# A decode kernel with two passes over a KV cache: the per-row layer chain as column products, cut into one-engine steps between K and V chunks

## The chip, the cores and the metric

One core of a Trainium2 chip runs the whole program. The metric is device time of one execution in microseconds (us), the median of several runs. A profile is one execution; its span is about 2 us shorter than the time of its run (1367.4 and 1369.2 us before). PE is the matmul engine (it loads weights, then multiplies), DVE the vector engine, ACT the scalar engine; a *pair* of instructions is one weight load and one matmul.

## The reference, cut to what matters

Eight rows (batch 8, one token each) pass through attention A, block B, attention A and block B again. Both attentions read the same caches, K and V, 134 MB each, so the work is reading them twice.

```
x = x + A(layernorm(x), k_cache, v_cache, wq, wo)   # 16 query heads, 8 KV heads, 4096 keys, head size 256
x = x + B(layernorm(x), ...)                        # for one token: x1 = x + 0 ; x1 + gelu(layernorm(x1) @ w3) @ w4
x = x + A(layernorm(x), k_cache, v_cache, wq, wo)
x = x + B(layernorm(x), ...)
```

D is 448, the MLP is 1792 wide, and q and the attention output are 4096 wide. With one token per row the mixing part of B is zero, so w1 and w2 are not used.

## The kernel before

The caches come in chunks of 1 MB (128 partitions of 8 KB) into six streaming slots; eight chunks per row (those of the last pair of KV heads) are kept in SBUF between the two passes. A task is one pass of one row over one pair of heads: four K chunks and four V chunks. A K chunk is transposed in place on DVE and multiplied with q on PE (32 load-and-matmul pairs); ACT takes the exponential of four chunks at once; a V chunk is multiplied with the transposed p (again 32 pairs). A slot is loaded again as soon as its chunk is used, so any stop of DVE or PE longer than the slots can cover is a stop of the loads (around the wo product of row 4, which keeps PE from 719.3 to 726.7 us, the rate is 401 GB/s in the window from 720 us and 164 in the next).

When a row's first pass is complete, its *chain* runs: normalize the attention output, product with wo, norm, MLP (w3, tanh gelu, w4), norm, q projection for the second pass, spread of q. The chain is a Python generator; each `next` emits one step among the chunks' instructions. The traces show the engines working in program order, so a step that waits holds up what is behind it: in that chain the scores of a chunk waited 2.87 us for its transpose, until 718.52 us, and the wo product behind them, whose input was complete at 716.2, began at 719.33.

```python
    def out_rows(lhs, w, n, b0, nb):            # n = 32 for wo, 14 for w4
        y_ps = ps_m.tile([nb, D], FP32, tag="m")
        for i in range(n):
            nc.tensor.matmul(y_ps[:], lhs(i), w[:, i, :], start=(i == 0), stop=(i == n - 1))
            if i % 16 == 15:
                yield
        y_sb = chn.tile([Bn, D], FP32, tag="y_sb")
        nc.scalar.copy(y_sb[:nb, :], y_ps[:])
        yield
        ps = rows_to_cols(y_sb, nb)             # five small transposing matmuls
        xs = xT[:, :, b0 : b0 + nb]
        nc.vector.tensor_add(xs, xs, ps[:])
    ...
    for idx, it in enumerate(items):            # K and V chunks, V four chunks behind K
        ...
        if kv == 0:
            transpose_k(slot); scores(...)      # exps after the fourth chunk
        else:
            pv(...)
        ...
        emit_loads()
        for _ in range(2):                      # two chain steps after every chunk
            for g in gens:
                next(g, None)
```

The softmax here doesn't subtract the row's maximum and nothing guards it: scores larger than these inputs give would overflow.

## Time and profile before

| | value |
|---|---|
| time | 1369.2 us, median of 4 (1367.8 to 1373.4) |
| bytes moved | 482.98 MB |
| rate away from the chains | 419 to 421 GB/s |
| bytes at 420 GB/s | 1150 us |
| lost in the first 65 us (weights) | 10 us |
| lost in eight chains | 168 us |
| lost after the last load (tail) | 39 us |

"Lost" is worked out everywhere in the same way: over 5-us windows, the sum of (420 - GB/s)/420 x 5 us, for each stretch in which the rate is below 420. Bytes at 420 GB/s plus what is lost gives the span.

These lines are from the profile's page of the kernel before: the mean DMA share in 40 equal slices (tenths), the rate in the same slices, the totals, and the chain of waits by engine and by line.

```profile
...
DMA  9999689599996999879996899959999599986980
GB/s 357 357 420 419 238 352 419 217 366 418 420 385 216 421 419 419 327 273 419 420 420 254 336 418 420 398 191 392 418 420 362 211 420 420 419 314 249 420 363 1
DMA packets 71816, 482.98 MB, mean 353 GB/s; under 512 B 7376, under 2 KB 13408, under 8 KB 13920
...
DMA 45%; PE 26%; DVE 21%; issue 3%; ACT 2%; SPq 2%; POOL 1%; POOLq 0%; DVEq 0%; ACTq 0%
DMA slot_103<-in_A_k_cache_dram 12%; DMA slot_106<-in_A_k_cache_dram 11%; DMA slot_115<-in_A_k_cache_dram 10%; PE y_ps L253 8%; DVE slot_103 L393 5%; DVE slot_107 L393 4%; DVE slot_105 L393 4%; PE sc_90 L400 4%; DMA slot_108<-in_A_v_cache_d
...
```

The rate is 420 in most slices and drops to between 190 and 275 once per row, eight times; the last slice moves next to nothing. Here are five of the 5-us windows of one such hole, the chain of row 4 (columns: window, length, then busy us and count for PE, weight loads, DVE, ACT, POOL, then PE clock, DMA share, GB/s).

```profile
...
720.00:725.00 5.00, 5.00 (x23) 2.03 (x22) 0.00 (x0) 0.00 (x0) 0.00 (x0) 0.81 0.97 401
725.00:730.00 5.00, 4.47 (x60) 3.23 (x58) 1.26 (x4) 0.52 (x1) 0.00 (x0) 1.00 0.51 164
...
735.00:740.00 5.00, 1.89 (x74) 1.88 (x71) 3.14 (x7) 0.21 (x1) 0.00 (x0) 0.50 0.74 306
...
745.00:750.00 5.00, 2.54 (x49) 2.43 (x49) 2.22 (x14) 0.00 (x0) 0.55 (x1) 0.92 0.21 31
...
760.00:765.00 5.00, 3.89 (x128) 3.44 (x128) 5.00 (x3) 0.00 (x0) 0.00 (x0) 0.50 0.70 242
...
```

Few windows have a full engine: PE from 720 on, DVE from 760 on, when it transposes what had piled up. The timeline of that moment has the 32 matmuls of the wo product with 448 columns, and the ACT copy behind them:

```profile
...
719.33 7.47 PE L253 MATMUL y_ps<-wo_sb,OT 128*1 128x448 bf16 x32
...
726.84 0.52 ACT L257 COPY y_sb<-y_ps 1x448 f32<-1x448 f32 x1 [12.52 <-PE y_ps L253]
...
```

And these are groups of instructions in the kernel before (line, engine, operation, output and inputs, shape, count, then busy us and mean ns). The q projection is already of the form that the change gives to the output products: 128-wide weights, one moving column.

```profile
...
L253 PE MATMUL y_ps<-wo_sb,OT 128*1 128x448 bf16 x256 | 62.1, 411 | 0.0
...
L253 PE MATMUL y_ps<-w_sb,HT 128*1 128x448 bf16 x112 | 32.9, 465 | 0.0
...
L298 PE MATMUL z_ps<-z_t,usel 128*128 128x4 f32 x128 | 29.6, 354 | 0.0
L219 PE MATMUL q_ps<-xb_99,wq_sb 128*128 128x1 bf16 x1024 | 28.6, 165 | 0.0
...
```

### The profile page before, as it was taken

How to read it: one execution, taken by the hardware profiler on the slowest of the kernel's cores; microseconds unless marked ns; L12 is line 12 of the kernel's file. 1: busy time of each engine (PE TensorE's matmuls, PEld its weight loads, DVE VectorE, ACT ScalarE, POOL GpSimd, SP SyncE). 2: the span in 40 equal slices, each digit the busy share in tenths (PEclk: the TensorE clock that was granted, in tenths of full speed). 3: DMA queues.
4: the chain of work that ended last, by engine and by line, in shares of the span. 5: the costliest groups of instructions: out<-in, count | busy, mean ns of one | idle time of the engine just before them, and what ended most of it. 6: DMA issues, size and time to landing. Idle time of an engine off the chain costs nothing.

```text
span 1367.4 us, 40957 instructions
## 1 busy us (share of the span) xinstructions
PE 749.1 (55%) x19436; PEld 610.0 (45%) x19436; DVE 582.4 (43%) x692; ACT 113.4 (8%) x220; POOL 15.3 (1%) x24
## 2 busy tenths in 40 slices
PE   3234665666355643666446754566536564476646
PEld 3234454455344543455334643355434453345533
DVE  4244345335435444345443364334543444434431
ACT  0000000000000100010000100000000010001000
POOL 0000000000000000000000000000000000000000
PEclk9999755655566555655557555565556555565556
DMA  9999689599996999879996899959999599986980
GB/s 357 357 420 419 238 352 419 217 366 418 420 385 216 421 419 419 327 273 419 420 420 254 336 418 420 398 191 392 418 420 362 211 420 420 419 314 249 420 363 1
DMA packets 71816, 482.98 MB, mean 353 GB/s; under 512 B 7376, under 2 KB 13408, under 8 KB 13920
## 3 DMA queue, kind: packets, MB, share of 16 engines
q1 hardware_dynamic: 71648, 480.36, 87.3%
q8 instruction: 152, 2.49, 0.7%
q14 instruction: 16, 0.13, 0.0%
HBM read 480.32 MB, written 0.01 MB: 351 GB/s over the span
## 4 chain that ended last, share of the span: by engine, by line
DMA 45%; PE 26%; DVE 21%; issue 3%; ACT 2%; SPq 2%; POOL 1%; POOLq 0%; DVEq 0%; ACTq 0%
DMA slot_103<-in_A_k_cache_dram 12%; DMA slot_106<-in_A_k_cache_dram 11%; DMA slot_115<-in_A_k_cache_dram 10%; PE y_ps L253 8%; DVE slot_103 L393 5%; DVE slot_107 L393 4%; DVE slot_105 L393 4%; PE sc_90 L400 4%; DMA slot_108<-in_A_v_cache_dram 3%; PE o_t L439 3%; PE sc_91 L400 3%; DMA slot_107<-in_A_v_cache_dram 3%; PE q_ps L219 2%; DVE slot_106 L393 2%; PE z_ps L298 2%
## 5 line engine op out<-in xcount | busy, mean ns | idle before, releaser
L400 PEld LDWEIGHTS <-qbd 128*8 128x8 bf16 x8192 | 203.5, 114 | 496.4 <-issue 419.9
L393 DVE STREAM_TRANSPOSE slot_103<-slot_103 128x2048 uint32<-128x2048 uint32 x64 | 147.6, 2306 | 107.7 <-DMA slot_103<-in_A_k_cache_dram 102.8
L393 DVE STREAM_TRANSPOSE slot_105<-slot_105 128x2048 uint32<-128x2048 uint32 x48 | 110.2, 2296 | 63.5 <-DMA slot_105<-in_A_k_cache_dram 63.5
L393 DVE STREAM_TRANSPOSE slot_107<-slot_107 128x2048 uint32<-128x2048 uint32 x48 | 110.2, 2296 | 47.5 <-DMA slot_107<-in_A_k_cache_dram 47.2
L400 PE MATMUL sc_91<-slot_103,qbd 128*8 128x128 bf16 x1408 | 44.7, 302 | 117.0 <-DVE slot_103 L393 115.8
L410 ACT ACTIVATE p_sb<-sc_91 128x512 bf16<-128x512 f32 x32 | 41.8, 1306 | 489.8 <-PE sc_91 L400 489.8
L439 PE MATMUL o_t<-pt,slot_108 128*128 128x2 bf16 x2048 | 64.7, 165 | 29.6 <-DMA slot_108<-in_A_v_cache_dram 23.2
L439 PEld LDWEIGHTS <-slot_108 128*128 128x128 bf16 x2048 | 59.3, 103 | 43.6 <-DMA slot_108<-in_A_v_cache_dram 25.2
L410 ACT ACTIVATE p_sb<-sc_90 128x512 bf16<-128x512 f32 x32 | 41.8, 1306 | 409.5 <-PE sc_90 L400 409.5
L307 DVE RECIPROCAL rz<-z_ps 128x16 f32<-128x16 f32 x16 | 4.1, 258 | 158.8 <-PE z_ps L298 158.8
L400 PE MATMUL sc_90<-slot_107,qbd 128*8 128x128 bf16 x960 | 31.4, 303 | 72.8 <-DVE slot_107 L393 68.7
L261 DVE TENSOR_TENSOR xT<-xT,ps 128x4 f32<-128x4 f32 (+1 forms) x18 | 3.0, 165 | 152.4 <-PE ps L150 152.4
L253 PE MATMUL y_ps<-wo_sb,OT 128*1 128x448 bf16 x256 | 62.1, 411 | 0.0
L400 PE MATMUL sc_91<-slot_105,qbd 128*8 128x128 bf16 x960 | 31.5, 303 | 52.7 <-DVE slot_105 L393 46.5
L439 PEld LDWEIGHTS <-slot_106 128*128 128x128 bf16 x1536 | 45.7, 104 | 15.7 <-issue 10.3
L439 PE MATMUL o_t<-pt,slot_106 128*128 128x2 bf16 x1536 | 48.8, 165 | 6.6 <-issue 3.4
L439 PEld LDWEIGHTS <-slot_104 128*128 128x128 bf16 x1536 | 44.7, 104 | 13.2 <-issue 9.7
L439 PE MATMUL o_t<-pt,slot_104 128*128 128x2 bf16 x1536 | 48.6, 166 | 2.9 <-DMA slot_104<-in_A_v_cache_dram 1.5
L393 DVE STREAM_TRANSPOSE slot_106<-slot_106 128x2048 uint32<-128x2048 uint32 x16 | 36.6, 2290 | 21.9 <-DMA slot_106<-in_A_k_cache_dram 21.9
L393 DVE STREAM_TRANSPOSE slot_104<-slot_104 128x2048 uint32<-128x2048 uint32 x16 | 36.6, 2290 | 20.0 <-DMA slot_104<-in_A_k_cache_dram 20.0
L253 PEld LDWEIGHTS <-OT 128*1 128x1 bf16 x256 | 24.7, 97 | 34.6 <-issue 16.3
L400 PE MATMUL sc_90<-slot_105,qbd 128*8 128x128 bf16 x576 | 18.4, 303 | 39.4 <-DVE slot_105 L393 17.6
(164 smaller groups left out, 878.4 us busy)
## 6 DMA issues: line engine op xcount, KB each, us to landing
slot_103<-in_A_k_cache_dram SPq DMA_DIRECT2D x64, 1024.0 KB, 9.7
slot_108<-in_A_v_cache_dram SPq DMA_DIRECT2D x64, 1024.0 KB, 13.7
slot_105<-in_A_k_cache_dram SPq DMA_DIRECT2D x48, 1024.0 KB, 11.4
slot_107<-in_A_k_cache_dram SPq DMA_DIRECT2D x48, 1024.0 KB, 12.5
slot_104<-in_A_v_cache_dram SPq DMA_DIRECT2D x48, 1024.0 KB, 10.6
slot_106<-in_A_v_cache_dram SPq DMA_DIRECT2D x48, 1024.0 KB, 11.7
slot_104<-in_A_k_cache_dram SPq DMA_DIRECT2D x16, 1024.0 KB, 14.0
slot_106<-in_A_k_cache_dram SPq DMA_DIRECT2D x16, 1024.0 KB, 19.9
```

What stands on the lines that cost most here:

```text
L219: nc.tensor.matmul(q_ps[:, j * Hq + h, :], w, xb[nb][:, xi, :], start=(fc == 0), stop=(fc == 3),)
L253: nc.tensor.matmul(y_ps[:], lhs(i), w[:, i, :], start=(i == 0), stop=(i == n - 1))
L261: nc.vector.tensor_add(xs, xs, ps[:])
L298: nc.tensor.matmul(z_ps[:, n, :], usel[:, n // 2, n % 2 : n % 2 + 1].to_broadcast([128, 128]), zall[:], start=True, stop=True,)
L307: nc.vector.reciprocal(rz[:], z_ps[:])
L393: nc.vector.transpose(w, w)
L400: nc.tensor.matmul(sc[32 * k : 32 * k + 8, 128 * x : 128 * x + 128], qbd[:, ep, gp].rearrange("p a h -> p (a h)"), kv[:, k, 2 * half + e2, ...
L410: nc.scalar.activation(p_sb[:].rearrange("p t i x -> p x t i"), sc[:].rearrange("p (x t i) -> p x t i", x=4, t=4), ACT.Exp, scale=scale_ex ...
L439: nc.tensor.matmul(o_ps[:, j, 2 * g : 2 * g + 2], v[:, y * Dh + 128 * j : y * Dh + 128 * j + 128], pt[:, y % 4, y // 4, 2 * a : 2 * a + 2] ...
```

## The change

Its intent is to make the chain shorter and to spread it, so that the loads do not stop, and to load one chunk per row less.

- The output products become columns with the weights stationary: no ACT copy, no transposes back. The last 64 columns of D are computed twice, since the layout of x holds them in both halves of the partitions.
- The chain is cut into more steps, each of which mainly uses one engine. One step goes between the K transpose and the scores, one before the V product, one after it. The chains of rows 0, 1, 6 and 7 take two steps at the first two places (five per K/V pair instead of three).
- V follows K by five chunks instead of four.
- The order of tasks leaves more tasks beside each chain.
- A ninth chunk per row is kept in SBUF.

```diff
-    kept = [(GP - 1, kv, n) for n in range(4) for kv in range(2)]
+    kept = [(GP - 1, kv, n) for n in range(4) for kv in range(2)] + [(GP - 2, 0, 0)]
...
-    def out_rows(lhs, w, n, b0, nb):
... (as shown above)
+    def out_cols(rhs, w, n, b0, nb, every):
+        y_ps = ps_m.tile([128, 4, nb], FP32, tag="m")
+        for fc in range(5):
+            lo, hi = (128 * fc, 128 * fc + 128) if fc < 3 else (384, 448)
+            r = y_ps[:, fc, :] if fc < 3 else y_ps[64 * (fc - 3) : 64 * (fc - 2), 3, :]
+            for i in range(n):
+                nc.tensor.matmul(r, w[:, i, lo:hi], rhs(i), start=(i == 0), stop=(i == n - 1))
+            if fc % every == every - 1 or fc == 4:
                 yield
         xs = xT[:, :, b0 : b0 + nb]
-        nc.vector.tensor_add(xs, xs, ps[:])
+        nc.vector.tensor_add(xs, xs, y_ps[:])
... (further yields in norm, the q projection and the MLP)
+    keep = sorted({gp for gp, _, _ in kept})
+    free = [gp for gp in range(GP) if gp not in keep]
+    tasks = [(0, 0, gp) for gp in free + keep] + [(0, 1, gp) for gp in free]
+    tasks += [(0, 2, free[0])]
+    for b in range(Bn):
+        tasks += [(1, b, gp) for gp in keep[::-1]]
+        if b + 1 < Bn:
+            tasks += [(0, b + 1, gp) for gp in keep]
+        if b == Bn - 2:
+            tasks += [(1, Bn - 3, free[-1])]
+        tasks += [(1, b, gp) for gp in (free[:-1] if b == Bn - 3 else free)]
+        if b + 2 < Bn:
+            tasks += [(0, b + 2, gp) for gp in (free[1:] if b == 0 else free)]
...
+    for j in range(nk + 5):
+        if j < nk:
+            items.append((j // 4, 0, j % 4))
+        if j >= 5:
+            items.append(((j - 5) // 4, 1, (j - 5) % 4))
...
+    def step(item=True):
+        for b, g in gens[:]:
+            for _ in range(2 if item and b in (0, 1, Bn - 2, Bn - 1) else 1):
+                if next(g, gens) is gens:
+                    gens.remove((b, g))
+                    break
...
                 transpose_k(slot)
+            step()
             scores(sc_t[n % 2], slot, c, st["q"], gp)
...
+            step()
             pv(state[ps, b]["o"], pt_of[n], slot, c, gp)
...
-        for _ in range(2):
-            for g in gens:
-                next(g, None)
+        if kv == 1:
+            step(False)
```

More of the change, by code (lines that the diff above doesn't have):

```diff
@@ L67 @@
     ps_s = ctx.enter_context(tc.tile_pool(name="ps_s", bufs=1, space=bass.MemoryType.PSUM))
-    ps_t = ctx.enter_context(tc.tile_pool(name="ps_t", bufs=2, space=bass.MemoryType.PSUM))
-    ps_o = ctx.enter_context(tc.tile_pool(name="ps_o", bufs=2, space=bass.MemoryType.PSUM))
+    ps_t = ctx.enter_context(tc.tile_pool(name="ps_t", bufs=1, space=bass.MemoryType.PSUM))
+    ps_o = ctx.enter_context(tc.tile_pool(name="ps_o", bufs=3, space=bass.MemoryType.PSUM))
     ps_m = ctx.enter_context(tc.tile_pool(name="ps_m", bufs=2, space=bass.MemoryType.PSUM))
@@ L141, in rows_to_cols @@
     def rows_to_cols(row, nb):
-        idn = ident[:nb, :nb]
+        idn = identb[:nb, :nb]
         ps = ps_m.tile([128, 4, nb], FP32, tag="m")
@@ L160, in norm @@
         nc.vector.tensor_mul(xs[:, :, 1, :], x, x)
+        yield
         st = ps_m.tile([128, 2, nb], FP32, tag="m")
@@ L225, in project_q @@
                     )
-            yield
+                if h % 8 == 7:
+                    yield
         nc.vector.tensor_copy(qT, q_ps[:])
+        yield
     def spread_q(qT, qbd):
@@ L247, in spread_q @@
             )
-    def out_rows(lhs, w, n, b0, nb):
-        y_ps = ps_m.tile([nb, D], FP32, tag="m")
-        for i in range(n):
-            nc.tensor.matmul(y_ps[:], lhs(i), w[:, i, :], start=(i == 0), stop=(i == n - 1))
-            if i % 16 == 15:
+    def out_cols(rhs, w, n, b0, nb, every):
[6 more added lines that the diff above has]
+            if fc % every == every - 1 or fc == 4:
                 yield
-        y_sb = chn.tile([Bn, D], FP32, tag="y_sb")
-        nc.scalar.copy(y_sb[:nb, :], y_ps[:])
-        yield
-        ps = rows_to_cols(y_sb, nb)
         xs = xT[:, :, b0 : b0 + nb]
-        nc.vector.tensor_add(xs, xs, ps[:])
+        nc.vector.tensor_add(xs, xs, y_ps[:])
     def mlp(b0, nb):
@@ L275, in mlp @@
                 )
+            if c == HC // 2:
+                yield
         yield
@@ L291, in mlp @@
         nc.vector.tensor_mul(HT[:].rearrange("p c b -> p (c b)"), g0[:], hx[:])
-        yield from out_rows(lambda c: HT[:, c, :], w4_sb, HC, b0, nb)
+        yield
+        yield from out_cols(lambda c: HT[:, c, :], w4_sb, HC, b0, nb, 3)
     def finish_attention(o_ps, zall, OT):
@@ L319, in chain @@
         yield from finish_attention(st["o"], st["z"], OT)
-        yield from out_rows(lambda i: OT[:, i % 2, i // 2 : i // 2 + 1], wo_sb, NB2, b, 1)
+        yield from out_cols(lambda i: OT[:, i % 2, i // 2 : i // 2 + 1], wo_sb, NB2, b, 1, 1)
         yield from mlp(b, 1)
@@ L329, in last @@
         yield from finish_attention(st["o"], st["z"], OT2[:, :, :, b])
-    first = [(0, gp) for gp in range(GP - 1)]
-    keep = GP - 1
-    tasks = [(0, 0, gp) for gp in range(GP)]
-    for b in range(1, Bn):
-        tasks += [(1, b - 2, gp) for gp in range(GP - 1)] if b > 1 else []
-        if b == 1:
-            tasks += [(0, 1, gp) for gp in range(GP - 1)]
-            tasks += [(1, 0, keep), (0, 1, keep)]
-        else:
-            tasks += [(1, b - 1, keep)]
-            tasks += [(0, b, gp) for gp in range(GP)]
-    if Bn > 1:
-        tasks += [(1, Bn - 2, gp) for gp in range(GP - 1)]
-    tasks += [(1, Bn - 1, keep)] + [(1, Bn - 1, gp) for gp in range(GP - 1)]
-    items = []
-    for n in range(len(tasks) + 1):
-        for c in range(4):
-            if n < len(tasks):
-                items.append((n, 0, c))
-            if n > 0:
-                items.append((n - 1, 1, c))
+    keep = sorted({gp for gp, _, _ in kept})
+    free = [gp for gp in range(GP) if gp not in keep]
+    assert Bn > 2 and len(free) > 1
+    tasks = [(0, 0, gp) for gp in free + keep] + [(0, 1, gp) for gp in free]
[9 more added lines that the diff above has]
+            tasks += [(0, b + 2, gp) for gp in (free[1:] if b == 0 else free)]
+    nk = 4 * len(tasks)
+    items = []
+    for j in range(nk + 5):
[3 more added lines that the diff above has]
+            items.append(((j - 5) // 4, 1, (j - 5) % 4))
     where, loads, r = {}, [], 0
@@ L408, in exps @@
     def exps(sc, zall, gp):
-        p_sb = work.tile([128, 4, 32, 4], BF16, tag="p_sb")
+        p_sb = work.tile([128, 4, 32, 4], BF16, tag="p_sb", bufs=1)
         nc.scalar.activation(
@@ L449 @@
     state = {}
-    x_row = chn.tile([Bn, D], BF16, tag="x_row")
-    nc.sync.dma_start(x_row[:], A_x.rearrange("b s d -> (b s) d"))
+    x_row = slots[-1][:Bn, :D]
+    nc.sync.dma_start(x_row, A_x.rearrange("b s d -> (b s) d"))
     emit_loads(2)
     load_split(wq_sb, A_wq, HD)
-    x_f = chn.tile([Bn, D], FP32, tag="y_sb")
-    nc.vector.tensor_copy(x_f[:], x_row[:])
-    ps0 = rows_to_cols(x_f, Bn)
+    ps0 = rows_to_cols(x_row, Bn)
     nc.vector.tensor_copy(xT[:], ps0[:])
@@ L462 @@
     gens, pairs_done, p_of, pt_of = [], {}, {}, {}
+    def step(item=True):
[4 more added lines that the diff above has]
+                    break
     late = False
+    late_steps = []
     for idx, it in enumerate(items):
@@ L471 @@
                     while (1, b) not in state:
-                        for g in gens:
-                            next(g, None)
+                        step()
+                        late_steps.append(b)
                 else:
@@ L485 @@
                 transpose_k(slot)
+            step()
             scores(sc_t[n % 2], slot, c, st["q"], gp)
+            if c == 0 and n > 0:
+                pt_of[n - 1] = transpose_p(p_of.pop(n - 1))
             if c == 3:
@@ L489 @@
         else:
+            if n in p_of:
+                pt_of[n] = transpose_p(p_of.pop(n))
+            step()
             pv(state[ps, b]["o"], pt_of[n], slot, c, gp)
@@ L493 @@
                 if pairs_done[ps, b] == GP:
-                    gens.append((chain if ps == 0 else last)(b, state.pop((ps, b))))
-        if n + 1 in p_of and kv == 1 and c == 3:
-            pt_of[n + 1] = transpose_p(p_of.pop(n + 1))
-        if n == 0 and kv == 0 and c == 3:
-            pt_of[0] = transpose_p(p_of.pop(0))
+                    gens.append((b, (chain if ps == 0 else last)(b, state[ps, b])))
         if not (ps == 0 and (gp, kv, c) in kept):
@@ L506 @@
             nc.sync.dma_start(w4_sb[:], B_w4.rearrange("(c p) d -> p c d", p=128))
-        for _ in range(2):
-            for g in gens:
-                next(g, None)
-    for g in gens:
+        if kv == 1:
+            step(False)
+    for _, g in gens:
         for _ in g:
             pass
-    for _ in out_rows(lambda i: OT2[:, i % 2, i // 2, :], wo_sb, NB2, 0, Bn):
+    for _ in out_cols(lambda i: OT2[:, i % 2, i // 2, :], wo_sb, NB2, 0, Bn, 5):
         pass
@@ L527 @@
         )
-    xo = chn.tile([Bn, D], BF16, tag="x_row")
-    nc.vector.tensor_copy(xo[:], o_row[:])
-    nc.sync.dma_start(out.rearrange("b s d -> (b s) d"), xo[:])
+    xo = slots[0][:Bn, :D]
+    nc.vector.tensor_copy(xo, o_row[:])
+    nc.sync.dma_start(out.rearrange("b s d -> (b s) d"), xo)
 _INS = ['A_x', 'A_k_cache', 'A_v_cache', 'A_wq', 'A_wo', 'B_x', 'B_w1', 'B_w2', 'B_w3', 'B_w4']
```

## The prediction

> **What bounds the kernel now.** DMA, with holes. The page shows 482.98 MB moved; away from the chains the 5-us windows show 413 to 426 GB/s at a DMA share of 1.00[...]. At 420 GB/s the bytes need 1150 of the 1367 us. The other 217 us, from windows: about 10 us in the first 60 us (329 to 399 GB/s, weight loads), 39 us after the last load (1328.5 to 1367.4), and about 168 us in eight holes. One hole: from 725 to 770 us the windows show 31 to 306 GB/s, a shortfall of 20 us. The timeline there shows one row's layer chain (out projection, norm, MLP, norm, q) from 714 to 759 us while only four K chunks pass: 10 us per K/V pair, where DMA needs 5.0. The streaming slots hide the first 7 us of each.
>
> **What the change does.**
> 1. Output products: 230 column matmuls instead of 46 of 448 columns. The timeline shows y_ps at 7.3 + 4.0 us, then an ACT copy (0.52) and transposes back (1.1) each: 14.5 us. The q projection already has the new form: 128 load-and-matmul pairs in 3.5 us, 27 ns each[...]. Estimate: 230 x 27 ns = 6.3 us, 8 us less.
> 2. Chain steps go between the 2.3 us K transposes on DVE and the scores, one engine per step. By program order a middle row's chain spreads over about 12 K chunks; those of rows 0, 1, 6, 7 over about 8. My sums of traced durations: 5 to 6 us per pair in middle chains; about 51 us for 8 pairs in the quick ones against 40 us of DMA, less 7 us hidden by slots. Loss: under 1 us per middle chain, 3 to 4 per quick one, about 14 in all; some 154 of 168 us come back. Program order forces no chain to its end before its row is needed.
> 3. One more kept chunk: eight loads and transposes fewer, 8.4 MB, 20 us at 420 GB/s, at full value, since DMA bounds.
> 4. V five chunks behind K: the exponential (1.57 us) and the transpose of p leave the path between chunks. Worth nothing where DMA bounds; it helps in chains.
> 5. Tail: out products of 8.5 and 4.6 us become about 4.4 and 1.9, copies and transposes go: 10 us less.
>
> **Sum.** 474.6 MB at 420 GB/s 1130; start 10; tail 29; chain losses 14: 1183. Range 1168 to 1215.
>
> **What would show it.** Right: in the 40 slices DMA at 9 nearly everywhere and about 420 GB/s in all but the first two, the last and perhaps four shallow ones; mean about 400 GB/s; DMA's share of the chain of waits far above 45%, y_ps (now 8%) off it; tail about 29 us. Step 2 is wrong if slices under 350 GB/s recur once per row; step 3 if MB falls but slices aren't full; step 5 if the tail stays over 35 us.
>
> **What would make it wrong.** Steps that serialize DVE and PE more than I summed (PE, in order, waits for a DVE step behind a transpose): 10 us a row gives 1230 to 1260. Loads blocked in order by a kept slot freed late: a new hole per row. A DMA rate that falls once it has no pauses: 1% per 4 GB/s.

## The result, and the profile after

The changed kernel took 1218.0 us (median of 4, 1217.6 to 1218.7), a ratio of 0.889 to the kernel before (95% interval 0.887 to 0.891). Ratios are the mean time of one kernel's runs over that of the other's of the same rounds, so they are not quite the ratio of the medians. The gain was right in kind, and 35 us smaller than predicted; the time lies 3 us outside the stated range.

The same lines of the page of the changed kernel:

```profile
...
DMA  9999989999999999999999999999999999998990
GB/s 347 365 403 419 419 318 398 420 419 357 397 419 420 398 405 415 419 418 382 408 420 420 382 409 418 419 420 389 413 408 420 401 357 394 419 417 339 411 404 3
DMA packets 70673, 474.75 MB, mean 390 GB/s; under 512 B 7248, under 2 KB 13280, under 8 KB 13792
...
DMA 44%; PE 30%; DVE 15%; issue 7%; SPq 3%; POOL 1%; ACT 0%; POOLq 0%; DVEq 0%; ACTq 0%
DMA slot_105<-in_A_k_cache_dram 10%; DMA slot_107<-in_A_k_cache_dram 10%; DMA slot_111<-in_A_k_cache_dram 9%; DMA slot_103<-in_A_k_cache_dram 8%; PE o_t L446 7%; PE y_ps L259 6%; PE sc_91 L407 5%; PE sc_90 L407 5%; DMA slot_104<-in_A_k_cach
...
```

| us | before | after | predicted |
|---|---|---|---|
| bytes at 420 GB/s | 1150.0 | 1130.4 | 1130 |
| lost at the start | 10.2 | 10.5 | 10 |
| lost in the chains of rows 0, 1, 6, 7 | 85.7 | 29.5 | 12 to 16 |
| lost in the chains of rows 2 to 5 | 82.1 | 14.0 | under 4 |
| lost in the tail | 38.8 | 31.5 | 29 |

The bytes, the start and the rate away from the chains are as foreseen. Of the miss, 30 us lie in the chains and 2.5 us in the tail. (Another profile of the changed kernel, after_again below, gives the same losses within 0.9 us per row.) DMA's share of the chain of waits did not rise (44%), against the prediction: PE still ends many waits.

Three windows of a middle chain (row 4), which before lost 20 us and now loses 3.5:

```profile
...
690.00:695.00 5.00, 2.42 (x86) 2.29 (x87) 4.54 (x11) 0.27 (x1) 0.38 (x1) 1.00 0.92 339
695.00:700.00 5.00, 4.92 (x168) 4.68 (x165) 4.47 (x8) 0.22 (x1) 0.00 (x0) 1.00 0.94 326
700.00:705.00 5.00, 3.02 (x84) 2.61 (x81) 2.62 (x4) 0.00 (x0) 0.00 (x0) 1.00 1.00 413
...
```

Three windows of a quick chain (row 6), which loses about 8:

```profile
...
970.00:975.00 5.00, 3.12 (x107) 2.84 (x105) 2.99 (x8) 1.33 (x3) 0.00 (x0) 1.00 0.70 262
975.00:980.00 5.00, 5.00 (x106) 4.75 (x104) 2.09 (x4) 0.27 (x1) 0.00 (x0) 1.00 0.99 375
...
985.00:990.00 5.00, 3.63 (x142) 3.29 (x133) 2.42 (x3) 0.00 (x0) 0.00 (x0) 1.00 0.66 226
...
```

The groups after, for comparison with those of before:

```profile
...
L220 PE MATMUL q_ps<-xb_99,wq_sb 128*128 128x1 bf16 x1024 | 30.3, 165 | 4.7 <-DVE xb_99 L208 4.7
L303 PE MATMUL z_ps<-z_t,usel 128*128 128x4 f32 x128 | 29.6, 354 | 0.0
...
L259 PE MATMUL y_ps<-OT,wo_sb 128*64 128x1 bf16 x512 | 29.1, 193 | 4.6 <-issue 4.6
...
L259 PE MATMUL y_ps<-OT,wo_sb 128*128 128x1 bf16 x768 | 23.7, 165 | 13.7 <-issue 7.8 <-DVE OT L314 5.9
...
```

A column pair has two prices. 768 matmuls with 128-wide weights are busy for 23.7 us, 31 ns each; 512 with 64-wide weights take 29.1 us, 57 ns each. The prediction had 27 for all.

A caution about the clock column: the windows of the change show 1.00 throughout, but its page has no line for the PE clock, and the durations say otherwise. The eight fp32 matmuls of a norm took 1.05 us in the kernel before at a granted clock of 1.00 (at 729.19 us) and take 1.87 us in the change (at 686.13 us); the fp32 matmuls of line 303 take 354 ns, exactly as the same ones (line 298) before, where the clock stood at 0.50 at one of them (713.8 us). So the clock of the change is unknown here, and nothing below rests on it.

In the timeline of the middle chain PE also stops inside a row of independent matmuls, with nothing that the trace says it waited for ("issue" in the brackets):

```profile
...
674.78 1.60 PE L259 MATMUL y_ps<-OT,wo_sb 128*128 128x1 bf16 x55
678.39 0.40 PE L259 MATMUL y_ps<-OT,wo_sb 128*128 128x1 bf16 x9 [2.00 <-issue]
678.72 1.03 PE L407 MATMUL sc_91<-slot_103,qbd 128*8 128x128 bf16 x32
...
682.42 1.38 PE L259 MATMUL y_ps<-OT,wo_sb 128*64 128x1 bf16 x23
684.60 0.64 PE L259 MATMUL y_ps<-OT,wo_sb 128*64 128x1 bf16 x9 [0.80 <-issue]
...
```

From 678.39 on, 9 + 32 + 32 + 32 + 23 = 128 matmuls follow until the next stop at 684.60 (the lines left out are counted in). 128 load-and-matmul pairs are 256 instructions. This became the first theory.

### The profile page after: what moved, and what is told of

Read it like the earlier page. It is cut to its first block, busy times and chain, and to the rows that moved or that the text cites. A ratio compares the mean times of both kernels' runs of the same rounds, so it can differ in the third digit from the quotient of the medians.

```text
span 1216.5 us, 43818 instructions
## 1 busy us (share of the span) xinstructions
PE 705.2 (58%) x20907; PEld 636.0 (52%) x20907; DVE 568.4 (47%) x683; ACT 103.5 (9%) x202; POOL 15.3 (1%) x24
## 4 chain that ended last, share of the span: by engine, by line
DMA 44%; PE 30%; DVE 15%; issue 7%; SPq 3%; POOL 1%; ACT 0%; POOLq 0%; DVEq 0%; ACTq 0%
DMA slot_105<-in_A_k_cache_dram 10%; DMA slot_107<-in_A_k_cache_dram 10%; DMA slot_111<-in_A_k_cache_dram 9%; DMA slot_103<-in_A_k_cache_dram 8%; PE o_t L446 7%; PE y_ps L259 6%; PE sc_91 L407 5%; PE sc_90 L407 5%; DMA slot_104<-in_A_k_cache_dram 3%; DVE slot_107 L400 3%; DVE slot_103 L400 3%; DVE slot_105 L400 3%; PE st L165 2%; DMA slot_115<-in_A_k_cache_dram 2%; PE q_ps L220 1%
## 5 line engine op out<-in xcount | busy, mean ns | idle before, releaser
L407 PEld LDWEIGHTS <-qbd 128*8 128x8 bf16 x8192 | 201.3, 115 | 366.2 <-issue 291.3
L400 DVE STREAM_TRANSPOSE slot_103<-slot_103 128x2048 uint32<-128x2048 uint32 x45 | 103.8, 2306 | 82.1 <-DMA slot_103<-in_A_k_cache_dram 79.3
L400 DVE STREAM_TRANSPOSE slot_105<-slot_105 128x2048 uint32<-128x2048 uint32 x44 | 101.5, 2307 | 58.5 <-DMA slot_105<-in_A_k_cache_dram 58.4
L400 DVE STREAM_TRANSPOSE slot_107<-slot_107 128x2048 uint32<-128x2048 uint32 x43 | 99.1, 2306 | 49.8 <-DMA slot_107<-in_A_k_cache_dram 49.6
L446 PE MATMUL o_t<-pt,slot_108 128*128 128x2 bf16 x1504 | 49.3, 166 | 41.4 <-DMA slot_108<-in_A_v_cache_dram 21.4
L446 PEld LDWEIGHTS <-slot_108 128*128 128x128 bf16 x1504 | 45.3, 105 | 49.4 <-issue 27.5
L259 PEld LDWEIGHTS <-wo_sb 128*128 128x128 bf16 (+1 forms) x1440 | 57.1, 125 | 22.5 <-issue 21.3
L259 PE MATMUL y_ps<-OT,wo_sb 128*128 128x1 bf16 (+1 forms) x1280 | 52.8, 176 | 18.3 <-issue 12.4
L400 DVE STREAM_TRANSPOSE slot_104<-slot_104 128x2048 uint32<-128x2048 uint32 x16 | 36.9, 2304 | 52.5 <-DMA slot_104<-in_A_k_cache_dram 52.4
L400 DVE STREAM_TRANSPOSE slot_108<-slot_108 128x2048 uint32<-128x2048 uint32 x14 | 32.3, 2306 | 60.8 <-DMA slot_108<-in_A_k_cache_dram 60.8
L446 PE MATMUL o_t<-pt,slot_106 128*128 128x2 bf16 x1504 | 48.5, 165 | 13.9 <-issue 13.2
L446 PEld LDWEIGHTS <-slot_106 128*128 128x128 bf16 x1504 | 45.2, 105 | 20.7 <-issue 19.7
L446 PE MATMUL o_t<-pt,slot_104 128*128 128x2 bf16 x1472 | 47.4, 165 | 13.7 <-issue 12.3
L446 PEld LDWEIGHTS <-slot_104 128*128 128x128 bf16 x1472 | 44.3, 105 | 20.3 <-issue 18.5
L400 DVE STREAM_TRANSPOSE slot_106<-slot_106 128x2048 uint32<-128x2048 uint32 x14 | 32.3, 2306 | 46.4 <-DMA slot_106<-in_A_k_cache_dram 46.3
L407 PE MATMUL sc_90<-slot_103,qbd 128*8 128x128 bf16 x800 | 26.3, 302 | 43.6 <-DVE slot_103 L400 33.6
L407 PE MATMUL sc_90<-slot_105,qbd 128*8 128x128 bf16 x768 | 24.8, 303 | 39.8 <-DVE slot_105 L400 31.1
L407 PE MATMUL sc_90<-slot_107,qbd 128*8 128x128 bf16 x704 | 22.8, 303 | 35.9 <-DVE slot_107 L400 27.2
L220 PEld LDWEIGHTS <-wq_sb 128*128 128x128 bf16 x1152 | 32.8, 104 | 19.2 <-DMA wq_sb<-in_A_wq_dram 10.7
L439 ACT CAST pt<-pt_ps 128x128 bf16<-128x128 f32 x64 | 17.0, 266 | 213.4 <-PE pt_ps L431 213.4
## 6 DMA issues: line engine op xcount, KB each, us to landing
slot_108<-in_A_v_cache_dram SPq DMA_DIRECT2D x47, 1024.0 KB, 12.1
```

What stands on the lines that cost most here:

```text
L220: nc.tensor.matmul(q_ps[:, j * Hq + h, :], w, xb[nb][:, xi, :], start=(fc == 0), stop=(fc == 3),)
L259: nc.tensor.matmul(r, w[:, i, lo:hi], rhs(i), start=(i == 0), stop=(i == n - 1))
L400: nc.vector.transpose(w, w)
L407: nc.tensor.matmul(sc[32 * k : 32 * k + 8, 128 * x : 128 * x + 128], qbd[:, ep, gp].rearrange("p a h -> p (a h)"), kv[:, k, 2 * half + e2, ...
L439: nc.scalar.copy(pt[:], pt_ps[:])
L446: nc.tensor.matmul(o_ps[:, j, 2 * g : 2 * g + 2], v[:, y * Dh + 128 * j : y * Dh + 128 * j + 128], pt[:, y % 4, y // 4, 2 * a : 2 * a + 2] ...
```

## The experiments

Each ran with the kernel before on the same chip (its median was 1367.8 to 1369.2 us on the chips used). Two theories for the 30 us in the chains were put against each other. **F**: PE's instructions arrive too slowly; while loads run, 256 instructions do not pass in less than about 6.1 us (read from the spacing of PE's stops; the two of the timeline above end 6.2 us apart). **S**: it is the working time of PE and DVE in the chain, one waiting for the other. The kernel after is the basis of each edit unless said otherwise. The losses of each run's chains, rows 0, 1, 6, 7 ("quick") and 2 to 5 ("middle") summed apart:

| run | time us | quick | middle | tail |
|---|---|---|---|---|
| the change | 1218.0 | 29.5 | 14.0 | 31.5 |
| after_again | 1219.9 | 29.8 | 12.4 | 31.5 |
| e_thin | 1259.5 | 54.5 | 31.0 | 31.7 |
| e_wide | 1236.3 | 47.3 | 12.1 | 31.4 |
| e_w128 | 1212.2 | 27.0 | 15.0 | 29.6 |
| e_leanwide | 1210.2 | 29.3 | 5.6 | 31.4 |
| e_kept8 | 1233.7 | 26.6 | 12.0 | 31.8 |
| e_rows8 | 1274.5 | 55.2 | 22.7 | 32.0 |
| e_lag4 | 1228.7 | 31.9 | 23.0 | 31.5 |
| e_step4 | 1217.3 | 30.0 | 12.8 | 31.2 |
| e_allquick | 1244.7 | 30.6 | 39.5 | 31.7 |
| e_slim | 1204.6 | 25.2 | 6.8 | 28.2 |
| e_best | 1205.1 | 26.1 | 7.0 | 29.1 |

### e_thin and e_wide: the same PE time, many or few instructions

```diff
                 if h % 8 == 7:
+                    for i in range(48 if nb == 1 else 0):      # e_wide: 4
+                        nc.tensor.matmul(q_all[:, 32 : 32 + 1],    # e_wide: 448 columns
+                            wq_sb[:, 128 * (i % 32) : 128 * (i % 32) + 128],
+                            wo_sb[:, i % 32, 0:1], ...)
                     yield
```

> 192 extra load-and-matmul pairs of one column in the q projection of each of the 8 row chains (4 times 48), results unused. Theory F (instruction fetch: while loads fill the DMA, PE cannot pass 256 instructions, which are 128 pairs, in less than about 6.1 us; read from the spacing of its unexplained stops): 192/128 x 6.1 = 9 us more per chain, little of it hidden, +45 to +75 us, and more stops of 1 to 2.4 us in the chains. Theory S (the working time of PE and DVE in the chain is what is missing): 192 x 29 ns = 5.6 us of PE per chain, at most +45 us, and as much as e_wide.

> The control of e_thin: 16 extra pairs of 448 columns per chain in the same places, about 0.375 us each at the low clock, so 6 us of PE per chain with 32 instructions instead of 384. F: clearly less than e_thin, +5 to +30 us. S: the same as e_thin or a little more.

The price of a wide pair shows in the trace of the kernel before: its 448-column matmuls start 0.373 us apart where the granted clock is 0.50 (1206 to 1209 us) and 0.189 us apart where it is 1.00 (722 to 726 us).

e_thin took 1259.5 us, 41 us more than the change; e_wide 1236.3, 18 us more. The 41 are a little below the range that F gave. The table says more: the extra matmuls were busy for about the same time (46.5 us in e_thin, 44.3 in e_wide); in the middle chains the many small pairs cost 17 us and the few large ones nothing, as F says; in the quick chains the large ones cost 18 us and the small ones 25, so there working time counts too, as S says.

### e_flood and e_floodw: the limit measured by itself

```diff
     def pv(...):                                # after each V chunk
+        for i in range(64):                     # e_floodw: 18
+            nc.tensor.matmul(o_ps[:].rearrange("p n h -> p (n h)")[:, 2 * Hq : 2 * Hq + 1],   # e_floodw: 128 columns
+                v[:, 128 * (i % 31) : 128 * (i % 31) + 128], ...)
```

> 64 extra one-column pairs after each V chunk, everywhere: 128 pairs per K/V pair instead of 64. F: one block of 256 instructions per K/V pair, so also away from chains a K/V pair takes about 6.1 us instead of 5.0, DMA falls to about 345 GB/s there, and the whole takes about 1600 us. S: PE works 2.0 + 1.9 us of each 5.0 us, so away from chains the rate stays 419 GB/s, and the whole stays under 1350.

> The control of e_flood: 18 extra pairs of 128 columns after each V chunk, about 1.9 us of PE at the low clock as there, but 36 instructions instead of 128. F: away from chains the rate is back at 419 GB/s, the whole 1225 to 1270. If PE working time made e_flood slow: about 1550.

e_flood took 1583.6 us, close to F's 1600. Its PE timeline, away from any wait for data:

```profile
...
460.24 0.96 PE L446 MATMUL o_t<-pt,slot 128*128 128x2 bf16 x30 [2.44 <-issue]
461.06 1.84 PE L455 MATMUL o_t<-slot 128*128 128x1 bf16 x64
462.83 1.02 PE L407 MATMUL sc<-slot,qbd 128*8 128x128 bf16 x32
463.79 0.21 PE L446 MATMUL o_t<-pt,slot 128*128 128x2 bf16 x2
466.45 0.96 PE L446 MATMUL o_t<-pt,slot 128*128 128x2 bf16 x30 [2.45 <-issue]
...
```

The stop of 2.4 us returns at the same place of the program, 128 pairs later: 460.24 to 466.45 is 6.21 us for 256 instructions. The pairs themselves took 3.8 us. Two of its windows, and two of e_floodw:

```profile
...
500.00:510.00 10.00, 6.82 (x255) 6.49 (x252) 6.71 (x16) 0.27 (x1) 0.70 (x1) 1.00 0.70 256
...
560.00:570.00 10.00, 8.77 (x307) 8.01 (x305) 4.63 (x3) 0.00 (x0) 0.00 (x0) 1.00 0.63 220
...
```

And the same columns for e_floodw:

```profile
...
510.00:520.00 10.00, 6.45 (x195) 5.80 (x195) 4.62 (x2) 1.32 (x2) 0.00 (x0) 1.00 1.01 417
...
550.00:560.00 10.00, 7.00 (x140) 6.19 (x138) 4.62 (x2) 1.32 (x2) 0.00 (x0) 0.50 1.01 418
...
```

With as much PE work per chunk (the added pairs are busy for 1.81 us on average in e_floodw, 1.84 at the place of e_flood shown above) but 36 added instructions instead of 128, seven of the 20 windows of 10 us from 440 to 640 us show 415 GB/s or more, against three in e_flood, and the time is 263 us shorter: e_flood was held up by the number of instructions. e_floodw as a whole took 1320.6 us, more than the 1225 to 1270 expected: its PE is 83% busy, and each chain lost 15 to 22 us. So PE time in a chain is not free either.

The traces also hold the loads of the instructions themselves, on a DMA queue of their own. These lines are from the pages of the change and of e_flood (queue, packets, MB, share of the DMA engines):

```profile
...
q8 instruction: 163, 2.67, 0.9%
...
```

```profile
...
q8 instruction: 291, 4.77, 1.2%
...
```

A packet is 16384 bytes, and in every run their number is PE's instructions divided by 256, rounded (41814 in the change, 74582 in e_flood: 163.3 and 291.3). The packed trace has the time of each. In the change, all 60 stops of PE of over 0.4 us that no other wait explains end 1.1 to 1.6 us after such a block has landed; in e_flood 159 of 163 do. So these stops are waits for instructions. Between two such stops the blocks start 6.1 us apart (median, loads at over 400 GB/s, in both runs); where the loads stood still in e_flood (under 15 GB/s), most came 3.3 to 3.8 us apart. The longer spacing went with a busy DMA. It is a median and not a floor: the change passed 247 pairs in the 10 us from 460 us at 422 GB/s, which is 5.2 us for 128.

### e_leanwide: fewer instructions at the same PE time (a wrong result on purpose)

```diff
-                for fc in range(4):              # q projection, and the first MLP product likewise
+                for fc in range(nf):             # nf = 2 in chains
...
+        if nb == 1:
+            n = n // 2                           # output products
+  (16 matmuls of 448 columns per chain, spread over the same steps, results unused)
```

> A wrong result on purpose. In the chains of single rows each output product, the q projection and the first MLP product sum only half of their contraction (207 pairs fewer per chain, 7.0 us of PE by the traced 27 to 56 ns), and 16 pairs of 448 columns, 6 us at the low clock, take their place step by step. So PE works about as long per chain, with some 380 instructions fewer; DVE and the steps are unchanged. Theory F (PE held up for instructions): the chain shortfalls, 43 us in the change, fall to 15 to 25 us, total 1190 to 1200. Theory S (working time of PE and DVE in the chain): they stay at 40 to 46 us, 1218 within 4 us.

1210.2 us. The middle chains fell from 14.0 to 5.6 us, the quick ones stayed at 29.3; the sum, 34.9 us, fits neither expectation. PE has 30 unexplained stops (47 us) instead of 60 (99 us). The rates in the 40 slices show it: of the slices 11 to 30 five are below 416 GB/s, against eleven in the change.

```profile
...
GB/s 345 370 403 420 418 313 391 420 419 351 392 421 420 418 419 418 419 411 399 418 419 421 395 420 419 420 419 398 416 416 420 396 355 421 419 417 349 405 404 2
...
```

PE was busy for the same time around the chain of row 3 (58.6 us in the 80 us from 530, in both kernels). So F makes most of the middle loss and nothing visible of the quick one. The comparison with the reference passed this kernel although it is wrong: the output products add little to x. For later edits of these products "correct" therefore says little; e_slimcheck deals with that.

### e_w128: the same number of instructions, less PE time

```diff
-            lo, hi = (128 * fc, 128 * fc + 128) if fc < 3 else (384, 448)
+                lo = (w0 + i) * D + (0, 128, 256, 384, 320)[fc]     # always 128 wide; half of the last two unused
```

> The two 64-wide blocks of the output products are loaded as 128-wide blocks of the same memory (the other half of the result is not used): the same number of PE instructions, but a pair should take 29 ns instead of 56. F: the chains stay as they are (each shortfall within 1 us), only the tail gets 2.4 us shorter: 1215 us. S: 2.4 us less in each chain too: about 1197 us. If a 128-wide block that does not start at a multiple of 128 columns is as slow as the 64-wide one, nothing changes at all.

1212.2 us. The pairs of the wo product took 31 ns each (1280 matmuls, 39.8 us busy) instead of 41 on average. The chains stayed within 2 us in sum (42.0 against 43.5) and the tail became 1.9 us shorter. The time fell by 6 us, of which the profile shows 4.

### e_kept8, e_lag4, e_rows8, e_beforecols: one part of the change alone or undone

```diff
 # e_kept8 (the order of tasks is held fixed)
-    kept = [...] + [(GP - 2, 0, 0)]
+    kept = [...]
-    keep = sorted({gp for gp, _, _ in kept})
+    keep = [GP - 2, GP - 1]
 # e_lag4
-    for j in range(nk + 5):
+    for j in range(nk + 4):
-        if j >= 5:
-            items.append(((j - 5) // 4, 1, (j - 5) % 4))
+        if j >= 4:
+            items.append(((j - 4) // 4, 1, (j - 4) % 4))
 # e_rows8: e_kept8, and in the chains (wo; w4 likewise)
-        yield from out_cols(lambda i: OT[...], wo_sb, NB2, b, 1, 1)
+        yield from out_rows(lambda i: OT[...], wo_sb, NB2, b, 1)
 # e_beforecols: the kernel before, in chains and at the end
-        yield from out_rows(lambda i: OT[...], wo_sb, NB2, b, 1)
+        yield from out_cols(lambda i: OT[...], wo_sb, NB2, b, 1, 1)
```

> The ninth kept chunk is loaded in both passes again; task order and all else as in the change. If DMA bounds where it is loaded: 8.4 MB at 420 GB/s, +20 us, 1238 us, in both theories. If its load falls where DMA has room (chains): +5 to +10 us.

> V follows K by four chunks instead of five, all else as in the change. The prediction gave this part nothing where DMA bounds. PE must then wait for the exponential and the copy of the transposed p (1.57 + 0.27 us and signals) before each task's first V product, in 64 tasks; hidden away from the chains by the slots: 1218 to 1226. If it were an important part: over 1235.

> To be compared with e_kept8 (1233.7), since the row form needs the room of the ninth chunk: the output products of the chains as rows of 448 columns again (46 pairs instead of 230, plus ACT copy and transposes), everything else as in e_kept8. Prediction's view: 8 us more chain, hidden in the middle chains, 3 to 5 us each in the four quick ones: about 1250. F: 368 instructions fewer per chain give back some 8 us of fetch time, so the two nearly cancel: 1228 to 1240. If the columns were the main gain of the change, 1270 or more.

> The kernel before with nothing changed but the column form of the output products. The prediction's sum: 8 us less per chain, all of it on the critical path there (a hole of 20 us each), and 10 us less tail: 1368 - 64 - 10 = about 1294. If the order of the steps, not their length, makes the hole: 1340 or more.

- e_kept8: 1233.7 us. The ninth chunk is worth 15.7 us, not the full 20. The trace of the change shows where the rest goes: once for each of rows 0 to 6 the queue of loads stops for 6.6 to 8.5 us in front of the load into the ninth chunk's slot, which is free only after its second use (for row 6 no load is issued between 998.9 and 1007.7 us), and then the rate dips (324 and 351 GB/s in the windows from 1005 and 1010 us). These dips lose about 7 us, 5.4 of them in rows 0, 1 and 6. e_kept8 has no such stop, and its chains lose 38.6 us in all against 43.5.
- e_lag4: 1228.7 us, so the lag is worth 11 us, more than expected. The line of waits that the change does not have to this size:

```profile
...
PE o_t L446 <- ACT pt L439: 17.0, 48, 0.4
...
```

  48 waits of 0.35 us are 17 us of PE; the middle chains, which have little to spare, lose 9 us more.
- e_rows8: 1274.5 us against 1233.7. The columns are worth 41 us in the new order, in both kinds of chain. My expectation under F, that the extra instructions would nearly cancel the gain, was wrong: the row form (in the kernel before a product of 7.5 us in one piece on PE, the ACT copy of 0.52, the transposes of 1.1) costs far more than 368 instructions. It also has fewer steps, so a middle chain stands beside 8 K chunks instead of 9; the two are not separated.
- e_beforecols: 1289.6 us, close to the 1294 of the prediction's sum. The column form alone brings 78 us (on its chip the kernel before took 1367.8); each hole shrinks from 19 to 23 us to 11 to 13, and the tail from 39 to 32. This is not the length of the products alone: the column form has more steps, so that 5 K chunks instead of 4 stand beside a chain (row 4: 41 us from its first product to the spread of q, 44 before).

### e_step4 and e_allquick: steps per pair, pairs beside a chain

```diff
 # e_step4 (step(2) stands before the scores, step() before the V product)
-            for _ in range(2 if item and b in (0, 1, Bn - 2, Bn - 1) else 1):
+            for _ in range(2 if item == 2 and b in (0, 1, Bn - 2, Bn - 1) else 1):
 # e_allquick
-            for _ in range(2 if item and b in (0, 1, Bn - 2, Bn - 1) else 1):
+            for _ in range(2 if item else 1):
```

> The chains of rows 0, 1, 6 and 7 take four steps per K/V pair instead of five (two before the scores, one before the V products, one after). F: their shortfall (9, 6, 8 and 6 us) is set by the instructions in the stretch, so it stays within 1 us each, 1218 within 4. If the crowding of steps within a pair causes it (S): 2 to 3 us less each, about 1208. If the chain then ends too late for its row: a new hole, 1225 or more.

> All rows take five steps per K/V pair, so the middle chains too stand beside 5 K chunks instead of 9. If the few pairs beside a chain make the loss (a chain of 38 us of work beside 6 pairs of 5 us, less 7 us hidden): the shortfall of each middle row rises from 3.5 to 6 to 9 us, total 1230 to 1240. If the place of the rows at the start and end makes it: 1218 within 4.

e_step4: 1217.3 us, no difference, though the quick chains now stand beside 6 K chunks instead of 5 (counted in the PE timeline) and take 40 to 43 us instead of 36 to 40. Rows 0 and 1 lost 12.3 instead of 15.1 us, rows 6 and 7 lost 17.7 instead of 14.4.

e_allquick: 1244.7 us. With five steps per pair, the program order of a middle chain has 5 score chunks between its first product (the z product of the normalization) and the spread of q, as in the quick rows, instead of 9. Its loss rises from 3.5 us per row to 9.9, and in the 40 slices the holes of rows 2 to 5 are back, while those of the other rows stay as they were:

```profile
...
GB/s 350 361 411 419 399 342 396 420 416 338 406 419 389 299 420 419 420 371 338 419 420 420 337 376 419 419 420 304 413 419 420 418 349 399 420 411 330 419 406 4
...
```

So it is the spread of the chain, five steps per pair beside 5 pairs against three beside 9, and not the row's place in the run, that makes a row lose more. The step from 5 to 6 pairs in e_step4 brought nothing, so the loss does not simply follow the count.

### e_half and e_quarter: smaller pieces per load

```diff
-            nc.sync.dma_start(dst[:], src)
+            w = 16 * Dh // 2                    # e_quarter: 4
+            for h in range(2):
+                nc.sync.dma_start(dst[:, h * w : h * w + w], src[:, h * w : h * w + w])
```

> Every 1 MB load is issued as two loads of half the row (4 KB pieces instead of 8 KB). Theory F has a finer form: [...] smaller pieces should shorten the 6 us. Then the stops of PE shrink (after: 60 stops over 0.4 us, 99 us in all) and the chain shortfalls fall from 43 us towards 25: about 1200 us. If the fetch time does not depend on the pieces, or theory S holds, the time stays within 4 us of 1218. If smaller pieces cost DMA rate, the stretches away from chains fall below 419 GB/s and the time rises.

> The same with four loads of 2 KB pieces. Finer form of F: stops shorter still, the chains lose 10 to 20 us, if the rate away from chains holds 419 GB/s: about 1195 us. Otherwise as e_half; the issue of four loads takes 4 x 0.33 us of 2.5 us per chunk, so the queue itself should not bound.

1256.7 and 1336.8 us. The finer form of F, which rested on a mechanism that no trace shows, fell for e_half: 69 stops of over 0.4 us, 120 us in all, against 60 and 99 us, and the instruction blocks came as far apart as before (6.2 us at over 400 GB/s). e_quarter has fewer stops (32, 38 us), but its loads are slower, so PE also needs fewer instructions per us; the two are not separated. In both runs the rate fell. The rates in the 40 slices of e_half:

```profile
...
GB/s 336 361 398 408 402 294 381 409 407 340 389 408 408 382 396 405 409 405 376 390 408 408 388 387 396 408 408 377 403 400 408 374 339 363 408 404 320 410 404 9
...
```

And those of e_quarter:

```profile
...
GB/s 322 347 376 386 381 323 359 385 370 351 379 348 373 367 365 362 370 383 382 383 380 372 369 364 363 381 375 378 354 378 383 383 334 370 346 372 348 367 378 35
...
```

Away from chains it is 408 GB/s with 4 KB pieces and at most 386 with 2 KB. These runs also issue two and four times as many loads, so whether the size of the pieces or the number of loads costs the rate is not separated (in the change, one issue takes 0.33 us on the queue). In the change the packet of a block is on the DMA for 1.0 us (median of 163); what the rest of the 6 us is spent on stays open.

### e_slim, e_best, e_slimcheck, after_again: a faster version

```diff
-        for fc in range(5):
-            lo, hi = (128 * fc, 128 * fc + 128) if fc < 3 else (384, 448)
+        for fc in range(4):
+            lo = 128 * fc if fc < 3 else 320
...
-            if fc % every == every - 1 or fc == 4:
+            if fc % every == every - 1 or fc == 3:
                 yield
+        nc.vector.tensor_copy(y_ps[0:64, 3, :], y_ps[64:128, 3, :])
 # e_best: e_slim, with e_step4's steps in rows 0 and 1
 # e_slimcheck: e_slim, and where x is brought into columns
-        for r in range(2):
+        for r in range(1, 2):
             nc.tensor.matmul(ps[64 * r : 64 * r + 64, 3, :], row[:nb, 384:448], idn, ...)
+        nc.vector.tensor_copy(ps[0:64, 3, :], ps[64:128, 3, :])
```

> A version that might beat both: the last 64 output columns are computed once, as a full 128-wide block ending at column 448 (its upper half is the wanted one), and DVE copies that half to the other partitions: 184 pairs per chain instead of 230, all 128 wide, one small DVE copy more per product. F: 46 pairs less are 2.2 us of fetch per chain, 10 to 16 us in all, and 3.5 us of tail: about 1201. S: as e_w128 showed, PE time in the chain is worth little: about 1212.

> e_slim (1204.6) with four steps per pair instead of five in rows 0 and 1 only, where e_step4 had lost 2.8 us less; rows 6 and 7, where it had lost 3 us more, keep five. About 1202; equal to e_slim if that was chance.

> e_slim, and the last 64 columns of the input x also reach partitions 0 to 63 only through the same DVE copy from partitions 64 to 127. If that copy were not what it seems, these columns of the output, which are mostly x, would be wrong and the comparison would fail. Expected: correct, time as e_slim, 1203 to 1207.

> The change itself, unaltered, on the same chip as e_slimcheck: 1216 to 1220, so 12 to 14 us above it.

e_slim: 1204.6 us; e_slimcheck: 1205.2, correct, so a copy between partitions of this form does what it should; after_again on the same chip: 1219.9. The slim version, as e_slimcheck, is 14.7 us faster than the change (ratios to before 0.880 and 0.891, intervals 0.878 to 0.882 and 0.889 to 0.893). It has 92 instructions fewer per chain and no 64-wide loads; the middle chains lose 6.8 us instead of 14.0, the quick ones 25.2, the tail 28.2. e_best is equal to it: the difference of e_step4 in rows 0 and 1 did not add.

## Why the prediction was right or wrong

- **"DMA, with holes"** was right: away from the chains the rate stayed at 419 to 420 GB/s. The table of bytes, holes and tail then adds up to the span by its definition: 1130.4 + 10.5 + 29.5 + 14.0 + 31.5 is 1216 us.
- **The columns (1)** were right as a mechanism and near in size where the chain bounds: 78 us in the old order with the tail (predicted 74). Part of that is luck: the holes gave 70 us instead of 64, helped by one more chunk beside each chain, and the tail 7 instead of 10. The size of a pair was wrong: 27 ns was read from the q projection, whose weights are all 128 wide. The 64-wide ones took 57 ns, so a chain's 230 pairs take 9.3 us instead of 6.3 (from the groups: 6.6 us for wo, 2.7 for w4). In the tail this is most of the miss (31.5 against 29; 29.6 in e_w128, where nothing but the width differs). In the chains it is worth under 2 us (e_w128).
- **The chains (2)** are the step that failed. It had "under 1 us per middle chain, 3 to 4 per quick one"; measured were 3.5 and 7.4. "A middle row's chain spreads over about 12 K chunks; those of rows 0, 1, 6, 7 over about 8" was misread from the program order: the order has 9 and 5. e_allquick shows the effect of the spread by itself: from 9 pairs to 5, the loss of the middle rows goes from 14.0 to 39.5 us.
- **The quick chains**, with their K and V work, take 36.4 to 39.8 us from the first product to the spread of q, beside 5 pairs, which DMA loads in 25; the prediction had 51 us for 8 pairs, 40 of DMA. By its own rule, 7 us of each hidden by the slots, that is 24 us of loss for the four rows. The stops in front of the ninth chunk's slot add 5.4 us: "loads blocked in order by a kept slot freed late", which the prediction listed as a risk, came true in small. Together 29.6 against 29.5 measured, but this is an estimate made afterwards: for the 6 pairs of e_step4 the same rule gives 17 us and those stops, and the measured loss was 30.0. Why a sixth pair brought nothing stays open.
- **Missing from the sum** was the arrival of PE's instructions, and this is what makes most of the middle rows' loss. With 9 pairs the middle chain needs 1014 pairs of load and matmul in program order; at 128 per 6.1 us that is 48 us, as an estimate, against 45 us of loads. e_leanwide takes 380 instructions away and the middle loss falls from 14.0 to 5.6 us. The estimate is rough: for e_thin it gives 12 us per middle row, which lost 8, and it does not explain e_slim, whose middle rows need 936 pairs beside 8 chunks and lost only 1.7 each. The prediction listed "PE, in order, waits for a DVE step" as the risk; that is the quick rows' share at most. There both limits lie close together: some 770 pairs at 128 per 6.1 us are 37 us, as an estimate, and the chain took 36 to 40, so fewer instructions alone (e_leanwide) could not show much.
- **The kept chunk (3)** "at full value" was a little wrong: 15.7 us of 20, because the loads, in order, stop in front of its slot once per row.
- **The lag (4)** "worth nothing where DMA bounds; it helps in chains" was right in kind; 11 us, of which 11.4 show in the chains.
- **The tail (5)** came to 31.5 instead of 29, by the 64-wide weights as said above.
- **The order of tasks and the placement of steps** together are what remains of the 151 us: 1289.6 (e_beforecols) minus 1218.0, less 15.7 for the chunk and 10.7 for the lag, leaves 45 us. This is a remainder, not a measurement.
- **"DMA's share of the chain of waits far above 45%"** was wrong as a sign: it is 44%. In the chain of waits a slot's load is preceded by the PE or DVE work that freed the slot, so the share of DMA does not tell how full it is (45% at a mean of 353 GB/s before, 44% at 390 after); the rate per slice does.

## What to carry to other kernels

Where loads bound, count what is lost against the full rate, stretch by stretch, and then count in the program order how many chunks really stand beside each piece of other work, on the engine that will be the tightest, before believing a sum. Turning a wide matmul into many one-column ones can shorten a chain a great deal, but it multiplies PE's instructions: look at how far apart every 128th pair is (here 6.1 us, between two stops of PE while loads ran at over 400 GB/s), and keep weight blocks 128 wide (31 ns a pair here, against 57 with blocks 64 wide). A comparison with the reference that a wrong kernel passes is no proof for an edit in that part; make the new operation carry something that the output depends on.
